# Gated attention and ReGLU block: the down products on exact 32-bit operands in four column tiles

## The chip, the cores and the metric

The kernel runs on one core of a Trainium2 chip. The metric is the time of one execution on the device in microseconds (us), the median of several runs. Five engines work side by side, each with its own instruction queue: PE (TensorE, matrix products; its weight loads are listed apart as PEld), DVE (VectorE), ACT (ScalarE), POOL (GpSimd) and SP (SyncE, which here only issues transfers). They meet through semaphores.

## The reference

For 2048 tokens of width 448 the result mixes an attention block (16 heads of width 28) and a gated feed-forward block (width 1792), token by token:

```python
x = A_x                                            # 1 x 2048 x 448
g = sigmoid((x * gate_w).sum(-1, keepdims=True))
qkv = (x @ wqkv).reshape(B, S, 3, H, Dh)           # H = 16, Dh = 28
p = softmax(einsum("bhqd,bhkd->bhqk", q, k) * Dh ** -0.5)
a = einsum("bhqk,bhkd->bhqd", p, v) ... @ wo
gate = einsum("bsd,df->bsf", x, W_gate)            # 448 -> 1792
up = einsum("bsd,df->bsf", x, W_up)
h = where(gate > 0, gate, 0) * up
b = einsum("bsf,fd->bsd", h, W_down)               # 1792 -> 448: the down products
out = g * a + (1 - g) * b
```

All arrays are 32-bit floats.

## The kernel before

The order of the instructions on every engine is written out by hand; no scheduler moves anything. The program has three stages.

**First stage.** Projections to q, k, v and the token gate, with x spilled to DRAM (`x_d`).

**Attention.** 32 rounds, two for each head. Each round follows a string of letters (`R0` to `R31`, listed in `ROUNDS`): `s` a pair of score products, `m` a pair of products for the row maxima, `x` one product of the feed-forward's gate or up projection (tile `gu`), `P` and `Q` the two halves of the products of P with V (function `pv`, tile `po`), and so on. `pv` works in *column tiles*: the stationary operand is a 128x32 piece of V, and four such products, one for each block of 512 tokens, write the partition rows 0 to 31, 32 to 63, 64 to 95 and 96 to 127 of one PSUM tile. P and V are 32-bit floats (F32) there. The feed-forward is spread under the attention: for every i (14 blocks f of 128 of the 1792 hidden columns, times 4 token blocks tb of 512; i = tb * 14 + f) the hidden tile h is computed as 128 hidden columns x 512 tokens and spilled to DRAM (`h_d`). The letter `D`, four times in the last two rounds, calls `split_wd`.

**Last stage** (after `stk.close()`). Four gate/up units that are left (`gate_up`), then for i = 0 to 55 the down products `down(i)`, accumulated over f into four PSUM tiles `ACC[tb][t]` of 128 tokens x 448; between them the output projection of the attention (`wout`, 11 products for each of the 16 token tiles t) and at each token block's end `result`, which mixes both parts and sends them out. A list `todo` sets the order of all engines here.

Most products use a *split*: an operand is divided into a high part, rounded to the type F32R, and the remainder (low), also F32R, and the product is formed as high x high, high x low, low x high. For the down products the table is

```python
PARTS = [(0, 0), (0, 1), (1, 0)]
```

so each (i, t) is three products of 128x128 stationary (h, one part) with 128x448 moving (weights, one part). The splits are extra work: `split_d(i)` makes `HH[i]` from the h tile (ACT the high part, line 136; DVE the low part, line 142), `split_wd(f)` does the same for the weights (ACT line 136, POOL line 145). The weights 0 to 3 are loaded and split early, in the last attention rounds, into the tiles K1 and K2; the weights 4 to 13 are fetched into `wdr` (4 places) by `fetch_w` and split into the tile `WD`. The h tiles 0 to 3 are also fetched early (tile `hk`, function `early_d`), the others by `fetch_h` into `hr` (4 places). All these fetches are issued by SP in program order. SP's issues use eight completion semaphores in turn, so an issue also waits until the transfer eight issues before it has landed.

Of the kernel before, what the change touches and what calls it, by code (L numbers as in the profile page):

```python
# [8 lines left out]
F32 = mybir.dt.float32  # L9
F32R = mybir.dt.float32r  # L10
# [8 lines left out]
P = 128  # L19
S = 2048  # L20
D = 448
H = 16
# [4 lines left out]
NF = F // P  # L27
NB = 4
TB = 512
# [62 lines left out]
QP = NL * NB * NT  # L92

BY_CHUNK = sorted(TERMS, key=lambda t: t[1] % 4)

PARTS = [(0, 0), (0, 1), (1, 0)]


@with_exitstack
def gated_mix_kernel(ctx, tc, x, wq, wo, wgu, wd, out):  # L100
    nc = tc.nc
# [7 lines left out]
    def f32(ap):  # L109
        return ap.bitcast(F32)  # L110
# [21 lines left out]
    def ps_x(name):  # L132
        return psum.tile([P, TB], F32, tag="x", bufs=2, name=name)

    def act_high(dst, src):
        nc.scalar.activation(dst, src, AF.Copy)  # L136
# [4 lines left out]
    def low(dst, src, high):  # L141
        nc.vector.tensor_tensor(dst, src, f32(high), op=OP.subtract)  # L142

    def pool_low(dst, src, high):
        nc.gpsimd.tensor_tensor(dst, src, f32(high), op=OP.subtract)
# [16 lines left out]
    V = vp.tile([P, 4, NK, 4, 32], F32, name="V")  # L162
    K = [(keep if r else vp).tile([P, S], F32R, name=f"K{r}") for r in range(3)]
# [42 lines left out]
    def rows_of(h):  # L206

        return [0 if j in raw(2 * h) else 1 if j in raw(2 * h + 1) else 2 for j in range(NB)]

    NU = [4 * sum(n > 0 for n in rows_of(h)) for h in range(H)]  # L210
    maxima = [(h, u, half) for h in range(H) for u in range(NU[h]) for half in range(rows_of(h)[u // 4])]
# [48 lines left out]
    stream = [p for v in range(2 * H) for p in visit(v)]  # L260
# [104 lines left out]
    with tc.tile_pool(name="qkv", bufs=1) as pa:  # L365
# [170 lines left out]
        m, first, ahead = 0, 6, MAXIMA  # L536
# [59 lines left out]
    done = (starts[-1] - QP) // (2 * NT)  # L596
# [127 lines left out]
        for j in range(4):  # L724
            nc.sync.dma_start(wo_d.rearrange("(g j d) n -> j d g n", j=4, d=DH)[j], wo[32 * j:32 * j + DH])

    DR, HK, early = {}, {}, []

    def wd_high_low(f, b):

        if f < 4:
            return K[1 + f // 2][:, (2 * (f % 2) + b) * D:(2 * (f % 2) + b + 1) * D]
        return WD[0][:, f - 4, b]

    def early_d():

        for i in range(0, 4, 2):
            h = fe.tile([P, 2, 4, P], F32, name=f"hk_{i}", tag="wgr", bufs=2).rearrange("p s c f -> p (s c f)")
            for k in range(2):
                DR[i + k] = V[:, 0].rearrange("p k h d -> p (k h d)")[:, (i + k) * D:(i + k + 1) * D]  # L740
                HK[i + k] = h[:, k * TB:(k + 1) * TB]
                nc.sync.dma_start(DR[i + k], wd[(i + k) * P:(i + k + 1) * P])
                nc.sync.dma_start(HK[i + k], h_d[i + k])

    def split_wd(i):

        r = DR.pop(i)
        act_high(wd_high_low(i, 0), r)
        pool_low(wd_high_low(i, 1), r, wd_high_low(i, 0))

    WD = []
    parts = 0
    passes = [(*divmod(k, 2), n) for k in range(-NL * NB, 2 * done) for n in range(NT)]
# [3 lines left out]
    def small_things(u):  # L757

        h, q = divmod(u, 4)

        if u in (22, 38):
            g = 2 if u < 32 else 3
            nc.sync.dma_start(V[:, g % 2], v_d[g])
        if u == 2:
            pack_wo()
        if h and q == 1:
            row_sums(h - 1)
            spread(h - 1)

    def loads(h, load):  # L770

        if 2 < h + 2 < H:
            load(h + 2)

    for v, order in enumerate(ROUNDS):
        small_things(2 * v)
        if v == 2 * H - 3:
            early_d()
        ns = 0
        for o in order:  # L780
            if o == "s":
                ns += 1
                if ns == 6:
                    small_things(2 * v + 1)
                if ns in (1, 9) and v % 2 == 0:
                    loads(v // 2, load_k if ns == 1 else load_q)
                if stream:
                    score()
            elif o == "m":
                if m < len(maxima):  # L790
                    smax(m)
                    m += 1
            elif o == "x":
                i, half, n = passes.pop(0)
                u = 2 * i + half + NL * NB
                if n == 0:
                    units.append(ps_x(f"qk_{u}" if i < 0 else f"gu_{i}_{half}"))
                if i < 0:
                    qk_mm(units[-1], u, n)
                else:  # L800
                    gu_mm(units[-1], i, half, n)
                if n == NT - 1:
                    ps = units.pop()
                    if half:
                        finished.add(i)
                    if i < 0:
                        send_qk(ps, NE + u % NL, u // NL, nc.sync)
                    elif half:
                        load_f(i + 2)
                        spill_h(i, ps)  # L810
                    else:
                        relu(i, ps)
            elif o == "n":
                if v % 2 and v < 2 * H - 1:
                    smax_end(v // 2 + 1)
            elif o == "w":
                ready = -(-max(0, starts[v + 2] - QP) // NT)
                ready = min(ready + ready % 2, 2 * NF)
                while parts < ready and parts // 2 - 2 in finished:
                    split_f(parts // 2, act_high, pool_low, (parts % 2,))  # L820
                    parts += 1
                    if parts % 2 == 0:
                        fetch_f(parts // 2 + 1)
            elif o == "b":
                block_min()
            elif o == "A":
                all_max()
            elif o == "g":
                take_max()
            elif o == "N":  # L830
                if v > 1 and v % 2:
                    normalise(v // 2 - 1)
            elif o in "eE":
                take_exp(o == "E")
            elif o in "cf":
                rescale(v, "cf".index(o))
            elif o == "D":
                split_wd(len(early))
                early.append(o)
            elif o in "PQ":  # L840
                pv(v, "PQ".index(o))
        rest = [k for k in todo_exp + todo_sub + todo_all if k[0] == v]
        assert not rest and v not in PO or len(stream) == max(0, 16 * (2 * H - 1 - v) - AHEAD), (v, passes, rest, len(stream) + 16 * (v + 1))
    assert not stream and not passes and m == len(maxima) and len(early) == 4, (len(stream), len(passes), m)
    stk.close()


# [1 line left out]
    pf = ctx.enter_context(tc.tile_pool(name="ffn", bufs=1))  # L849
# [12 lines left out]
        act_high(WO[:, 6], r[:, 3])  # L862
        low(WO[64:, 6], r[64:, 3], WO[64:, 6])

    ON, OR, GA, HH, ACC = {}, {}, {}, {}, {}

    def fetch_o(tb):
        OR[tb] = r = pf.tile([P, 4, TB], F32, name=f"or_{tb}", tag="or", bufs=1)
# [32 lines left out]
        relu(i, ps[:, 0])  # L901
        spill_h(i, ps[:, 1])

    WD.append(pf.tile([P, NF - 4, 2, D], F32R, name="WD"))

    def fetch_w(i):

        if i < NF:
            DR[i] = pf.tile([P, D], F32, name=f"wdr_{i}", tag="wdr", bufs=4)
            nc.sync.dma_start(DR[i], wd[i * P:(i + 1) * P])  # L910

    def fetch_h(i):

        if i < NB * NF:
            HK[i] = pf.tile([P, TB], F32, name=f"hr_{i}", tag="hr", bufs=4)
            nc.sync.dma_start(HK[i], h_d[i])

    def split_d(i):
        HH[i] = pf.tile([P, 2, TB], F32R, name=f"hh_{i}", tag="hh", bufs=3)
        h = HK.pop(i)  # L920
        act_high(HH[i][:, 0], h)
        low(HH[i][:, 1], h, HH[i][:, 0])

    def down_mm(i, t):
        f = i % NF
        for n, (a, b) in enumerate(PARTS):
            nc.tensor.matmul(ACC[i // NF][t][:, :D], HH[i][:, a, t * P:(t + 1) * P], wd_high_low(f, b),  # L927
                             start=(f == 0 and n == 0), stop=(f == NF - 1 and n == 2))

    def result(tb, t, queue):  # L930
        k = tb * 4 + t
# [8 lines left out]
    def down(i):  # L940
# [6 lines left out]
        if f == NF - 1:  # L947
# [5 lines left out]


    wor = []
    todo = [(fetch_w, 4), (fetch_h, 4), (fetch_w, 5), (fetch_h, 5), (split_d, 0), (row_sums, H - 1), (split_d, 1),
            (fetch_w, 6), (fetch_w, 7), (lambda: wor.append(load_wo()),), (fetch_h, 6), (gate_up, done), (spread, H - 1),
            (split_wd, 4), (fetch_w, 8), (split_wd, 5), (fetch_w, 9), (fetch_h, 7), (gate_up, done + 1)]
    for i in range(NB * NF):
        if 5 < i + 3 < NF:  # L960
            todo += [(split_wd, i + 3), (fetch_w, i + 7)]
        if i + 2 < NB * NF:
            todo.append((split_d, i + 2))
        if i >= 2:
            todo.append((fetch_h, i + 6))
        todo.append((down, i))
        if i % 2 == 0 and 2 < i and done + i // 2 < NB * NF:
            todo.append((gate_up, done + i // 2))
# [54 lines left out]
```

## Time and profile before

| | before |
|---|---|
| median of 3 runs | 1184.81 us (1184.59 to 1185.01) |
| profiled execution, its own time | 1184.21 us |
| its span, first to last instruction | 1182.4 us |
| granted TensorE clock, mean | 0.999 |
| DMA, mean over the span | 160 GB/s |
| last stage, from the first `gate_up` product to the last down product | 985.76 to 1178.6 us |

The span is what the trace's rows add up to; the execution's own time is 1.8 us more, before the first and after the last instruction. In the page and in the answers on the trace, "PE MATMUL acc<-WD,hh 128*128 128x448 f32 x480 | 99.5, 366" means: 480 products that write tile acc from tiles WD and hh, stationary 128x128, moving 128x448, together busy 99.5 us, one lasting 366 ns from its start to its end. Products overlap in the pipeline, so the pace is read from the starts of successive ones in the timeline and not from that duration.

### The profile page before, as it was taken

The page shows a single profiled execution, that of the slowest core. Times are in us where ns is not written, and L with a number is a line of the kernel's source. Part 1 is how long each engine was busy: PE and PEld are TensorE (multiplying, and loading weights), DVE is VectorE, ACT ScalarE, POOL GpSimd, SP SyncE. Part 2 cuts the span into 40 slices and gives each one's busy share as a digit, 9 for nine tenths or more (in the row PEclk, how much of TensorE's full clock was granted, in tenths as well). Part 3 has the DMA queues.
Part 4 walks back from the last instruction along what each step waited for, and adds up shares of the span by engine and source line. Part 5 has one row for each costly group of instructions (what it writes and reads, how often), then busy time and mean ns, then how long its engine had stood idle before and what let it go on. Part 6 is the DMA issues. An engine that isn't in the chain of part 4 may idle for free.

```text
span 1182.4 us, 17006 instructions
## 1 busy us (share of the span) xinstructions
PE 1175.0 (99%) x6183; PEld 821.2 (69%) x6183; DVE 894.1 (76%) x1173; ACT 877.2 (74%) x1054; POOL 743.3 (63%) x325
## 2 busy tenths in 40 slices
PE   9999999999999999999999999999999999999998
PEld 6886666666666666666666666666666667899997
DVE  6577898888988898989898888889898553444242
ACT  5237889899999988888888887888888885322121
POOL 5323667888988886777777766767676784422020
PEclk9999999999999999999999999999999999999999
DMA  9994565636373754343446535153444437644342
GB/s 322 280 394 142 186 210 172 185 124 196 117 216 108 205 167 139 119 128 92 119 136 212 140 102 153 49 152 109 139 154 156 129 100 231 209 152 118 115 134 75
DMA packets 70667, 188.85 MB, mean 160 GB/s; under 512 B 13958, under 2 KB 20558, under 8 KB 65678
## 3 DMA queue, kind: packets, MB, share of 16 engines
q1 hardware_dynamic: 65624, 167.31, 45.9%
q0 software_dynamic: 4480, 19.99, 4.5%
q8 instruction: 48, 0.79, 0.3%
q10 hardware_dynamic: 480, 0.47, 0.1%
q14 instruction: 35, 0.29, 0.1%
HBM read 126.96 MB, written 60.96 MB: 159 GB/s over the span
## 4 chain that ended last, share of the span: by engine, by line
PE 96%; DVE 1%; DMA 1%; ACT 1%; issue 0%; SPq 0%; DVEq 0%; ACTq 0%
PE gu L633 24%; PE s L330 20%; PE po L692 19%; PE acc L927 12%; PE sm L224 10%; PE v L469 3%; PE wo L886 3%; PE qk L641 3%; PE qk L454 2%; DVE r L280 1%; DMA wr<-wq 0%; DMA X<-x_d 0%; ACT P L336 0%; ACT V L336 0%; SPq L414 0%
## 5 line engine op out<-in xcount | busy, mean ns | idle before, releaser
L309 POOL TENSOR_TENSOR P<-P,rm 128x2048 f32<-128x2048 f32 x102 | 470.8, 4635 | 107.9 <-DVE rm L303 84.1
L633 PE MATMUL gu<-X,wg 128*128 128x512 f32 x1232 | 358.9, 395 | 0.1
L228 DVE TENSOR_REDUCE mx<-sm 128x1 f32<-128x1024 f32 x256 | 302.9, 1217 | 43.0 <-PE sm L224 42.1
L330 PE MATMUL s<-Q,K 128*128 128x512 f32 x1024 | 315.9, 403 | 1.7 <-DVE mx L228 0.9
L633 PEld LDWEIGHTS gu<-X,wg 128*128 128x128 f32 x1232 | 231.2, 188 | 57.6 <-issue 1.7
L330 PEld LDWEIGHTS s<-Q,K 128*128 128x128 f32 x1024 | 180.7, 188 | 82.4 <-DVE r L280 10.4
L336 ACT ACTIVATE P<-s 128x1024 f32<-128x1024 f32 x204 | 202.2, 1028 | 42.0 <-PE s L330 39.6
L692 PE MATMUL po<-P,V 128*32 128x512 f32 x1640 | 227.4, 594 | 0.0
L334 ACT ACTIVATE P<-s 128x1024 f32<-128x1024 f32 x206 | 201.4, 1040 | 14.1 <-PE s L330 13.1
L320 ACT ACTIVATE P<-P 128x1024 f32<-128x1024 f32 (+1 forms) x182 | 208.5, 1171 | 0.5 <-POOL P L309 0.2
L224 PE MATMUL sm<-K,Q 128*128 128x512 f32 x520 | 163.2, 400 | 0.1
L280 DVE SCALAR_TENSOR_TENSOR r<-s,r 128x1024 f32<-128x1024 f32 x124 | 151.6, 1223 | 13.6 <-ACT P L336 6.0
L692 PEld LDWEIGHTS po<-P,V 128*32 128x32 f32 x1640 | 62.6, 110 | 113.3 <-issue 109.6
L692 PE MATMUL po<-V 128*32 128x512 f32 x408 | 136.2, 594 | 0.0
L309 POOL TENSOR_TENSOR V<-V,rm 128x2048 f32<-128x2048 f32 x24 | 111.2, 4635 | 26.1 <-DVE rm L303 22.6
L224 PEld LDWEIGHTS sm<-K,Q 128*128 128x128 f32 x520 | 91.9, 188 | 34.1 <-ACT P L334 4.6
L136 ACT ACTIVATE hh<-hr 128x512 fp32r<-128x512 f32 x52 | 32.8, 632 | 109.5 <-PE acc L927 109.4
L142 DVE TENSOR_TENSOR hh<-hr,hh 128x512 fp32r<-128x512 f32 x52 | 47.3, 915 | 72.6 <-ACT hh L136 72.5
L927 PE MATMUL acc<-WD,hh 128*128 128x448 f32 x480 | 99.5, 366 | 0.0
L927 PEld LDWEIGHTS acc<-WD,hh 128*128 128x128 f32 x480 | 90.2, 188 | 7.3 <-DVE hh L142 0.2
L280 DVE SCALAR_TENSOR_TENSOR r<-s,P 128x1024 f32<-128x1024 f32 x50 | 61.1, 1223 | 33.3 <-ACT P L336 33.0
L295 DVE TRANSPOSE_TENSOR_REDUCE mn<-r 128x32 f32<-128x1024 f32 x63 | 78.1, 1239 | 1.3
(93 smaller groups left out, 1135.5 us busy)
## 6 DMA issues: line engine op xcount, KB each, us to landing
wg<-ws_d SPq DMA_DIRECT2D x42, 896.0 KB
K<-qk_d SPq DMA_DIRECT2D x32, 448.0 KB
X<-x_d SPq DMA_DIRECT2D x56, 256.0 KB
h_d<-h SPq DMA_DIRECT2D x56, 256.0 KB
Q<-qk_d SPq DMA_DIRECT2D x62, 224.0 KB
hr<-h_d SPq DMA_DIRECT2D x52, 256.0 KB
ws_d<-wg SPq DMA_DIRECT2D x14, 896.0 KB
x_d<-X POOLq DMA_DIRECT2D x8, 1024.0 KB, 15.2
```

Of the source, the lines that this page charges most:

```text
L224: nc.tensor.matmul(ps[:, c, :], Q[h][:, u * P:(u + 1) * P], K[h % 3][:, k0:k0 + TB], start=True, stop=True)
L228: nc.vector.tensor_reduce(to, ps, axis=AX.XY, op=OP.max)
L280: nc.vector.scalar_tensor_tensor(r, ps, -1.0, before, op0=OP.mult, op1=OP.min)
L295: nc.vector.tensor_reduce(MN[:, 1:3], R2.pop((v, j)).rearrange("p a (b r) -> p a b r", r=32), axis=AX.X, op=OP.min, apply_transpose=True)
L309: nc.gpsimd.tensor_tensor(QUAD[q], QUAD[q], m, op=OP.subtract)
L320: nc.scalar.activation(q, q, AF.Exp, scale=-SCALE)
L330: nc.tensor.matmul(ps[:, c], K[h % 3][:, k * P:(k + 1) * P], Q[h][:, j * TB:(j + 1) * TB], start=True, stop=True)
L334: nc.scalar.activation(dst, ps, AF.Exp, scale=SCALE)
L336: nc.scalar.activation(dst, ps, AF.Copy, scale=-1.0)
L633: nc.tensor.matmul(ps, WS[i][:, s, a], xf(i // NF, b), start=(n == 0), stop=(n == NT - 1))
L692: nc.tensor.matmul(po[32 * j:32 * j + 32], V[:, h // 4 % 2, k, h % 4], AT.pop((v, k, j)), start=(k == k0), stop=(k == k0 + NK // 2 - 1))
L927: nc.tensor.matmul(ACC[i // NF][t][:, :D], HH[i][:, a, t * P:(t + 1) * P], wd_high_low(f, b), start=(f == 0 and n == 0), stop=(f == NF - 1 ...
```

## The change

Both operands of the down products stay whole 32-bit floats (F32). Nothing is split: `PARTS`, `split_d`, `split_wd` and the tiles `HH` and `wdr` are gone. Each (i, t) becomes four products, one for each group of 32 tokens, with a 128x32 stationary piece of h and the 128x448 moving weights of block f; they write the partition rows 0, 32, 64 and 96 onwards of the same PSUM tile. The weights 0 to 3 are no longer fetched in the attention rounds; all 14 are fetched straight into `WD` in the last stage, 0 to 3 first of all. `hr` has eight places where there were four.

```diff
-PARTS = [(0, 0), (0, 1), (1, 0)]
...
-    def wd_high_low(f, b):
-
-        if f < 4:
-            return K[1 + f // 2][:, (2 * (f % 2) + b) * D:(2 * (f % 2) + b + 1) * D]
-        return WD[0][:, f - 4, b]
+    def wd_rows(f):
+
+        return WD[0][:, f]
...
-                DR[i + k] = V[:, 0].rearrange("p k h d -> p (k h d)")[:, (i + k) * D:(i + k + 1) * D]
                 HK[i + k] = h[:, k * TB:(k + 1) * TB]
-                nc.sync.dma_start(DR[i + k], wd[(i + k) * P:(i + k + 1) * P])
                 nc.sync.dma_start(HK[i + k], h_d[i + k])
-
-    def split_wd(i):
-
-        r = DR.pop(i)
-        act_high(wd_high_low(i, 0), r)
-        pool_low(wd_high_low(i, 1), r, wd_high_low(i, 0))
...
-            elif o == "D":
-                split_wd(len(early))
-                early.append(o)
...
-    WD.append(pf.tile([P, NF - 4, 2, D], F32R, name="WD"))
+    WD.append(pf.tile([P, NF, D], F32, name="WD"))
...
-            DR[i] = pf.tile([P, D], F32, name=f"wdr_{i}", tag="wdr", bufs=4)
-            nc.sync.dma_start(DR[i], wd[i * P:(i + 1) * P])
+            nc.sync.dma_start(wd_rows(i), wd[i * P:(i + 1) * P])
...
-            HK[i] = pf.tile([P, TB], F32, name=f"hr_{i}", tag="hr", bufs=4)
+            HK[i] = pf.tile([P, TB], F32, name=f"hr_{i}", tag="hr", bufs=8)
...
-    def split_d(i):
-        HH[i] = pf.tile([P, 2, TB], F32R, name=f"hh_{i}", tag="hh", bufs=3)
-        h = HK.pop(i)
-        act_high(HH[i][:, 0], h)
-        low(HH[i][:, 1], h, HH[i][:, 0])
 
     def down_mm(i, t):
         f = i % NF
-        for n, (a, b) in enumerate(PARTS):
-            nc.tensor.matmul(ACC[i // NF][t][:, :D], HH[i][:, a, t * P:(t + 1) * P], wd_high_low(f, b),
-                             start=(f == 0 and n == 0), stop=(f == NF - 1 and n == 2))
+        for k in range(0, P, 32):
+            nc.tensor.matmul(ACC[i // NF][t][k:k + 32, :D], HK[i][:, t * P + k:t * P + k + 32], wd_rows(f), start=(f == 0),
+                             stop=(f == NF - 1))
...
-    todo = [(fetch_w, 4), (fetch_h, 4), (fetch_w, 5), (fetch_h, 5), (split_d, 0), (row_sums, H - 1), (split_d, 1),
+    todo = [(fetch_w, 0), (fetch_w, 1), (fetch_w, 2), (fetch_w, 3), (fetch_w, 4), (fetch_h, 4), (fetch_w, 5), (fetch_h, 5), (row_sums, H - 1),
...
-            todo += [(split_wd, i + 3), (fetch_w, i + 7)]
-        if i + 2 < NB * NF:
-            todo.append((split_d, i + 2))
+            todo.append((fetch_w, i + 7))
```

On PE the same place in the program, `down(1)`, reads as follows; `acc_0` to `acc_3` are the four PSUM tiles of the token block, `hh` the split h, `K_105` the early split weights. Before:

```order
L927 MATMUL acc_0_9059<-K_105,hh_8966 128x448 [waits Activation_49]
L927 MATMUL acc_0_9059<-K_105,hh_8966 128x448
L927 MATMUL acc_0_9059<-K_105,hh_8966 128x448 [waits DVE_49]
L927 MATMUL acc_1_9060<-K_105,hh_8966 128x448 x3
L927 MATMUL acc_2_9061<-K_105,hh_8966 128x448 x3
L927 MATMUL acc_3_9062<-K_105,hh_8966 128x448 x3
```

With the change (`hk` is the unsplit h tile, fetched early):

```order
L905 MATMUL acc_0_9032<-WD,hk_8257 32x448 [waits DMAHW1_49]
L905 MATMUL acc_0_9032<-WD,hk_8257 32x448 x3
L905 MATMUL acc_1_9033<-WD,hk_8257 32x448 x4
L905 MATMUL acc_2_9034<-WD,hk_8257 32x448 x4
L905 MATMUL acc_3_9035<-WD,hk_8257 32x448 x4
```

Twelve products that waited for ACT and DVE have become sixteen narrow ones that wait only for the weights' transfer.

On SP's queue the start of the last stage is reordered; `ls` is the last head's row sums, `l_d` sends them back, `wor` is the output projection's weights. Before:

```order
L702 DMA ls_8939<-ox 128x1x16 [waits DMAHW3_49,DVE_49]
L910 DMA wdr_8952<-wd 128x448 [waits DMAHW4_49,PE_49,Pool_49]
L916 DMA hr_8954<-h_d_2606 128x512 [waits DMAHW5_49]
L910 DMA wdr_8956<-wd 128x448 [waits DMAHW6_49]
L916 DMA hr_8958<-h_d_2768 128x512 [waits DMAHW7_49]
L708 DMA l_d_97<-rq_8963 128x16 [waits DMAHW0_49,DVE_49]
```

With the change:

```order
L700 DMA ls_8927<-ox 128x1x16 [waits DMAHW7_49,DVE_49]
L894 DMA WD<-wd 128x448 [waits DMAHW0_49,PE_49,Activation_49]
L894 DMA WD<-wd 128x448 [waits DMAHW1_49]
L894 DMA WD<-wd 128x448 [waits DMAHW2_49]
L894 DMA WD<-wd 128x448 [waits DMAHW3_49]
L894 DMA WD<-wd 128x448 [waits DMAHW4_49]
L900 DMA hr_8945<-h_d_2606 128x512 [waits DMAHW5_49]
L894 DMA WD<-wd 128x448 [waits DMAHW6_49]
L900 DMA hr_8948<-h_d_2768 128x512 [waits DMAHW7_49]
L706 DMA l_d_97<-rq_8950 128x16 [waits DMAHW0_49,DVE_49]
```

Four weight transfers stand ahead of everything that was there. The first waits for PE, that is for the last product of P with V, whose operand V lay where `WD` now begins.

More of the change, by code (lines that the diff above doesn't have):

```diff
@@ L725, in pack_wo @@
             nc.sync.dma_start(wo_d.rearrange("(g j d) n -> j d g n", j=4, d=DH)[j], wo[32 * j:32 * j + DH])
-    DR, HK, early = {}, {}, []
-    def wd_high_low(f, b):
-        if f < 4:
-            return K[1 + f // 2][:, (2 * (f % 2) + b) * D:(2 * (f % 2) + b + 1) * D]
-        return WD[0][:, f - 4, b]
+    HK = {}
+    def wd_rows(f):
+        return WD[0][:, f]
     def early_d():
@@ L843, in gated_mix_kernel @@
         assert not rest and v not in PO or len(stream) == max(0, 16 * (2 * H - 1 - v) - AHEAD), (v, passes, rest, len(stream) + 16 * (v + 1))
-    assert not stream and not passes and m == len(maxima) and len(early) == 4, (len(stream), len(passes), m)
+    assert not stream and not passes and m == len(maxima), (len(stream), len(passes), m)
     stk.close()
@@ L863, in split_wo @@
         low(WO[64:, 6], r[64:, 3], WO[64:, 6])
-    ON, OR, GA, HH, ACC = {}, {}, {}, {}, {}
+    ON, OR, GA, ACC = {}, {}, {}, {}
     def fetch_o(tb):
@@ L955, in gated_mix_kernel @@
     wor = []
-    todo = [(fetch_w, 4), (fetch_h, 4), (fetch_w, 5), (fetch_h, 5), (split_d, 0), (row_sums, H - 1), (split_d, 1),
+    todo = [(fetch_w, 0), (fetch_w, 1), (fetch_w, 2), (fetch_w, 3), (fetch_w, 4), (fetch_h, 4), (fetch_w, 5), (fetch_h, 5), (row_sums, H - 1),
             (fetch_w, 6), (fetch_w, 7), (lambda: wor.append(load_wo()),), (fetch_h, 6), (gate_up, done), (spread, H - 1),
-            (split_wd, 4), (fetch_w, 8), (split_wd, 5), (fetch_w, 9), (fetch_h, 7), (gate_up, done + 1)]
+            (fetch_w, 8), (fetch_w, 9), (fetch_h, 7), (gate_up, done + 1)]
     for i in range(NB * NF):
         if 5 < i + 3 < NF:
-            todo += [(split_wd, i + 3), (fetch_w, i + 7)]
-        if i + 2 < NB * NF:
-            todo.append((split_d, i + 2))
+            todo.append((fetch_w, i + 7))
         if i >= 2:
```

## The prediction

> **What bounds the kernel now.** I read the page's busy shares and the chain first. The chain is the work that ended last, followed back; its second row splits its share by line.
>
> ```profile
> PE 1175.0 (99%) x6183; PEld 821.2 (69%) x6183; DVE 894.1 (76%) x1173; ACT 877.2 (74%) x1054; POOL 743.3 (63%) x325
> ...
> PE 96%; DVE 1%; DMA 1%; ACT 1%; issue 0%; SPq 0%; DVEq 0%; ACTq 0%
> PE gu L633 24%; PE s L330 20%; PE po L692 19%; PE acc L927 12%; PE sm L224 10%; PE v L469 3%; PE wo L886 3%; PE qk L641 3%; PE qk L454 2%; DVE r L280 1%; DMA wr<-wq 0%; DMA X<-x_d 0%; ACT P L336 0%; ACT V L336 0%; SPq L414 0%
> ```
>
> PE is the chain nearly throughout, and the down products (`acc`, line 927) are 12% of it. Since an average can hide a stage with another limit, I then asked for busy time in two stretches, the last stage and all before it; the columns are length, then each engine's busy time and instructions, clock, DMA share and GB/s.
>
> ```profile
> 985.76:1178.60 192.84, 192.81 (x940) 175.86 (x936) 78.43 (x100) 51.34 (x81) 38.90 (x31) 1.00 0.48 150
> 0.00:985.76 985.76, 982.20 (x5248) 645.39 (x5248) 815.02 (x1072) 825.87 (x973) 704.41 (x295) 1.00 0.51 162
> ```
>
> In the last stage PE is busy 192.81 of 192.84 us, at a granted clock of 1.00; DVE is busy 78.43 and ACT 51.34 of these. So whatever changes PE's work there changes the end by as much, and work taken from DVE, ACT or POOL gives nothing. Before that stage PE lacks 3.56 us in all, so taking the four early splits away can give at most that and, as the splits are 8 small instructions among thousands, I take 0. The last question is how long PE takes for a product of each kind.
>
> **The products that go.** The groups by line, with their shapes, give the count: 480 + 192 = 672 products of 128x448.
>
> ```profile
> L927 PE MATMUL acc<-WD,hh 128*128 128x448 f32 x480 | 99.5, 366 | 0.0
> L927 PE MATMUL acc<-K,hh 128*128 128x448 f32 x192 | 39.6, 365 | 0.0
> ...
> L142 DVE TENSOR_TENSOR hh<-hr,hh 128x512 fp32r<-128x512 f32 x52 | 47.3, 915 | 72.6 <-ACT hh L136 72.5
> L136 ACT ACTIVATE hh<-hr 128x512 fp32r<-128x512 f32 x52 | 32.8, 632 | 109.5 <-PE acc L927 109.4
> ```
>
> The pace stands in the timeline (start, time covered, engine, count), where down products alternate with the equally shaped `wo` products:
>
> ```profile
> 1059.16 2.40 PE L886 MATMUL wo<-WO,on 128*128 128x448 f32 x11
> 1061.40 2.60 PE L927 MATMUL acc<-WD,hh 128*128 128x448 f32 x12
> 1063.83 2.39 PE L886 MATMUL wo<-WO,on 128*128 128x448 f32 x11
> ```
>
> From 1059.16 to 1063.83 PE starts 23 products: 4.67 / 23 = 0.203 us each. Gone from PE: 672 x 0.203 = **136.4 us**. The splits of h go too (52 x 0.632 on ACT, 52 x 0.915 on DVE, and four more of each for the early tiles), but both groups' idle columns show the splits waiting, ACT for PE and DVE for ACT: they run ahead of PE and were never what it waited for. Their gain is 0.
>
> **The products that come.** 56 h tiles x 4 token tiles x 4 column tiles = 896 products of 128x32 stationary with 128x448 moving, both 32-bit. The trace has their like: the products of P with V are 128x32 with 128x512, both F32, four column tiles in turn. One line's view, and one `P`+`Q` run in the timeline from the product before it to the one after:
>
> ```profile
> L692 PEld LDWEIGHTS po<-P,V x1640: 105/110/111, 114.0 to 984.8; 128*32 128x32 f32 x183
> L692 PE MATMUL po<-P,V x1640: 592/592/618, 114.0 to 985.2; 128*32 128x512 f32 x183
> L692 PEld LDWEIGHTS po<-V x408: 106/110/111, 117.0 to 984.8; 128*32 128x32 f32 x136
> L692 PE MATMUL po<-V x408: 592/592/617, 117.4 to 985.2; 128*32 128x512 f32 x136
> ...
> 617.73 0.62 PE L330 MATMUL s<-Q,K 128*128 128x512 f32 x2
> 618.19 0.39 PE L633 MATMUL gu<-X,wg 128*128 128x512 f32 x1
> ...
> 620.13 1.08 PE L330 MATMUL s<-Q,K 128*128 128x512 f32 x4
> 621.15 0.62 PE L692 MATMUL po<-P,V 128*32 128x512 f32 x2
> ...
> 621.61 0.59 PE L692 MATMUL po<-V 128*32 128x512 f32 x1
> ...
> 627.61 0.61 PE L692 MATMUL po<-P,V 128*32 128x512 f32 x3
> ...
> 628.15 1.20 PE L330 MATMUL s<-Q,K 128*128 128x512 f32 x4
> ```
>
> The code has 32 visits x 8 k x 4 j = 1024 such products; the view counts 1640 + 408 = 2048, so the hardware runs each 32-bit product as two loads and two products. In the timeline they come in sets of four records, one for each column tile, side by side; a visit's half-head has 64 records, 16 sets, and the first starts at 621.15 and the last at 627.61: 6.46 / 15 = 0.431 us a set (neighbouring sets show 0.43). Four products of 512 columns thus take two sets, 0.861 us.
>
> How this shrinks to 448 columns the trace does not show. If a set is streaming of its columns, it becomes 0.431 x 448 / 512 = 0.377; if it is a fixed cost (loads, issue), it stays 0.431. The full-array products decide which is nearer: 512 columns take (618.19 - 617.73) / 2 = 0.230, 448 take 0.203, which is 0.88 of it against 448 / 512 = 0.875. Time goes with columns there, and a set of 0.431 is two passes of 512 at 0.215, a little under the full array's 0.230, so it has even less fixed cost. I take **0.377**. The lower bound is the pace without the first set, 627.61 - 621.61 over 14 or less, 0.428 x 0.875 = 0.375; the upper is 0.431.
>
> 224 (i, t) x 2 sets x 0.377 = **168.9 us**, with bounds 168.0 and 193.1.
>
> A rule of the Trainium skill, page "FP8 and Floating Point Precision", section TensorE Precision Notes, bears on this: a true FP32 product takes 4 passes through the array. The trace agrees, as two sets of 0.431 are four times 0.215. Priced with the full array's pass of 448 instead, that rule gives 224 x 4 x 0.203 = 181.9 and so 13 us more; since the column-tiled pass is measured the shorter, the set stands.
>
> **Switching between full array and column tiles.** Into the run: four `s` from 620.13 at 0.230 would be over at 621.05, and `po` starts at 621.15, 0.10 later. Out of it: the last set's start plus 0.431 is 628.04, the next product starts at 628.15, 0.11 later. In the program the down products stand in 13 unbroken pieces: 13 x 0.10 + 12 x 0.11 = **2.6 us**, which were not there (the alternation at 1061.40 shows no such gap). Bounds 0 and twice that.
>
> **The moved loads.** Rows 0 to 3 of the weights are now fetched in the last stage, behind the row sums `ls`; the first waits for the last product with V. Order and landing of the like before:
>
> ```profile
> 985.76 3.07 PE L633 MATMUL gu<-X,wg 128*128 128x512 f32 x12
> ...
> 986.84 0.61 SPq L702 DMA_DIRECT2D ls<-ox  x1
> 987.55 0.41 SPq L910 DMA_DIRECT2D wdr<-wd  x1
> ...
> 996.17 1.18 PE L927 MATMUL acc<-K,hh 128*128 128x448 f32 x5
> ...
> wdr<-wd SPq DMA_DIRECT2D x10, 224.0 KB
> ...
> L136 ACT ACTIVATE WD<-wdr x10: 559/567/579, 991.7 to 1029.1; 128x448 fp32r<-128x448 f32 x10
> ...
> 986.20:996.20 10.00, 10.00 (x45) 8.04 (x44) 2.79 (x5) 2.79 (x5) 3.39 (x3) 1.00 0.94 315
> ```
>
> PV ends and `gate_up` begins at 985.76, so that wait is over before `ls` is issued; row 0 takes the place of the transfer issued at 987.55, which was used at 991.7 at the latest. PE needs it at 996.17: 4.5 us to spare, hidden by the two `gate_up`. Rows 1 to 3 follow in four issues of 0.41 to 0.47 and are needed 3 us apart. What is queued behind is later by 4 x 224 KB at 315 GB/s, about 2.9 us: the h tiles 4 and 5, `l_d`, `wor`, the weights of the third `gate_up`, which PE needs only after `down(4)`. There PE also arrives later, by 5 x (2 x 4 x 0.377 - 12 x 0.203) = 2.9 us, as much as the transfers. Cost 0; if the cover failed, at most some 4 us (a transfer queued wholly behind, and its landing). The eight places of `hr` are refilled when a `down` has freed one, so h is fetched six `down`, some 18 us, ahead, and a fetch has no longer to wait for a split.
>
> **The end.** The last product, one DVE mix and one transfer are as before:
>
> ```profile
> 1178.61 0.68 DVE L933 SCALAR_TENSOR_TENSOR y<-acc,gate,ga 128x448 f32<-128x448 f32 x1 [0.53 <-PE acc L927]
> 1179.32 0.36 ACTq L935 DMA_DIRECT2D out<-y  x1
> ```
>
> DVE needs 0.68 for a token tile; PE gives it one each 1.22 now and each 4 x 0.377 = 1.51 then. Nothing is added.
>
> **Sum.** -136.4 + 168.9 + 2.6 = +35.1 us. On the profiled execution's own time, 1184.21 (span 1182.4), that is 1219.3; the median of the runs is 0.6 higher, 1184.81, which gives **1219.9 us**.
>
> **The rivals.**
>
> *The sets do not shrink.* A set is held at 0.431 by something that does not go with columns. The widths above speak against it, though no 448-column set is in the trace. 193.1 + 2.6 - 136.4 = +59.3: 1244. Between lies a set whose passes each pay the full array's 0.203: 448 x 2 x 0.203 = 181.9, +48.1, 1233.
>
> *The weight loads come out from under the products.* A set needs four loads of 0.110 (row above). If one such time were exposed in each set because here each column tile has other weights, while the four tiles of PV load the same piece of V: 448 x 0.110 = 49.3 more, 1269. The timeline speaks against it: the loads are made in PV too, and 0.431 leaves no room beside two passes' worth of streaming. The Trainium skill, page "TensorE: Matmul & The Clock Gate", section The mechanism, states that weight loads overlap running products only where the row groups differ. By that rule all column tiles, which share their rows, would expose their loads; the PV sets, 0.431 with loads of 0.110 in it, do not bear it out, and I give it little.
>
> *A transfer is late at the start of the stage*, by the 4 us above: 1224.
>
> *Faster.* The four tiles of a set read the same weights here and four different tiles of P in PV. If PV's pace were that of reading its moving operands, a shared one could go up to four times as fast. It decides from 136.4 - 2.6 = 133.8 / 448 = 0.299 us a set down; at half the pace, 0.19, the sum is 85.1 + 2.6 - 136.4 = -48.7, 1136. Against it: a pass of 512 takes 0.215 there, while the full array, with one moving operand, takes 0.230; PV is not slower than one stream, so a shared one has nothing to gain.
>
> **How the numbers follow.** Sets that shrink with the columns, everything hidden: 0.83. Late transfer: 0.04. No shrinking, or the full array's pass: 0.07. Exposed loads: 0.02. Faster: 0.03; something that balances it: 0.01. 0.2%, 2.4 us, is about what a measurement of this kernel can tell from no change. So slower 0.96, same 0.01, faster 0.03. The range: below, the set at 0.375, no switching cost and the 3.56 us of early idle returned, -136.4 + 168.0 - 3.56 = +28.0, 1212.8; above, the forecast with switching doubled, the late transfer and half of the way to the full array's pass, 1219.9 + 2.6 + 4 + 6.5 = 1233.
>
> **What would show it.** The line of the down products should count 1792 records of 128x32, in sets 0.377 apart, 3.02 us for one `down`, and the last stage should last 192.8 + 35.1 = 228 us. Sets at 0.43 show the second case; sets near 0.49 the loads; a gap on PE ahead of the first `down` or of the third `gate_up` the transfers. ACT and DVE should be nearly idle there. The prediction is wrong if a set is not what a set in PV is: same form, but other weights in each tile and one moving operand for all four.

## The result and the profile after

The changed kernel takes 1221.85 us, median of 4 runs (1220.68 to 1222.16), against 1184.91 us (1184.59 to 1186.27) for the kernel before in the same set of runs: a ratio of 1.0308 (1.029 to 1.0326), 36.9 us more. The forecast was 1219.9 us. The profiled execution after took 1220.68 us with a span of 1218.8 us, 36.4 us more than the span before.

The page's busy times, and the chain by engine and by line:

```profile
span 1218.8 us, 19006 instructions
...
PE 1211.4 (99%) x7303; PEld 750.6 (62%) x7303; DVE 844.6 (69%) x1117; ACT 836.5 (69%) x984; POOL 723.4 (59%) x311
...
PE 96%; ACT 1%; DVE 1%; DMA 1%; issue 0%; SPq 0%; ACTq 0%; DVEq 0%
PE gu L631 23%; PE s L328 19%; PE po L690 18%; PE acc L905 14%; PE sm L222 10%; PE wo L871 3%; PE v L467 3%; PE qk L639 3%; PE qk L452 2%; DVE r L278 1%; DMA wr<-wq 0%; ACT P L334 0%; DMA v_d<-V 0%; ACT P L332 0%; ACT V L334 0%
```

DVE lost 49.5 us of work, ACT 40.7, POOL 19.9, and none of it came back in the time: PE was the chain before and is the chain after, and PE's busy time rose by 36.4 us, from 1175.0 to 1211.4, as much as the span. The down products' share of the chain rose from 12% to 14%. The windows of the last stage, and of its first five `down`, show no hole on PE, and PE's own list of waits in this stage has no row (columns: length, then busy time of PE, PEld, DVE, ACT and POOL with their instructions, clock, DMA share, GB/s):

```profile
985.56:1214.40 228.84, 228.84 (x2060) 105.50 (x2056) 29.10 (x44) 12.30 (x15) 21.95 (x19) 1.00 0.41 130
996.06:1011.23 15.17, 15.17 (x161) 5.10 (x160) 3.48 (x6) 2.50 (x4) 1.28 (x1) 1.00 0.98 326
```

The answer on the line of the down products has 1664 + 128 = 1792 records, as forecast:

```profile
L905 PE MATMUL acc<-WD,hr x1664: 539/539/564, 1008.1 to 1214.4; 128*32 128x448 f32 x185
L905 PE MATMUL acc<-WD,hk x128: 539/539/563, 996.1 to 1007.8; 128*32 128x448 f32 x128
```

The timeline around one `down` between two `wo` runs gives the pace. The four weight loads that go with a set show when the set starts:

```profile
1035.62 1.69 PE L905 MATMUL acc<-WD,hr 128*32 128x448 f32 x16
1037.24 2.50 PE L871 MATMUL wo<-WO,on 128*128 128x448 f32 x11
1039.67 3.21 PE L905 MATMUL acc<-WD,hr 128*32 128x448 f32 x32
1042.82 0.47 PE L871 MATMUL wo<-WO,on 128*128 128x448 f32 x1
...
1040.07 0.13 PEld L905 LDWEIGHTS acc<-WD,hr 128*32 128x32 f32 x4 [0.25 <-issue]
1040.45 0.13 PEld L905 LDWEIGHTS acc<-WD,hr 128*32 128x32 f32 x4 [0.25 <-issue]
1040.82 0.13 PEld L905 LDWEIGHTS acc<-WD,hr 128*32 128x32 f32 x4 [0.25 <-issue]
```

From 1040.07 to 1040.82 there are two sets; in the trace's nanoseconds they start 0.376 apart (0.377 was forecast). The `down` from 1039.67 to 1042.82 takes 3.15 us, 0.14 more than its eight sets of 0.376, and the run of 11 `wo` from 1037.24 to 1039.67 takes 2.43 us where 11 x 0.203 = 2.23 were needed before. So each change from full array to column tiles and back costs 0.20 + 0.14 = 0.34 us, where 0.21 was forecast.

### The profile page after: what moved, and what is told of

The parts are those of the page before. It is cut to its first block, busy times and chain, and to the rows that moved or that the text cites. A ratio compares the mean times of both kernels' runs of the same rounds, so it can differ in the third digit from the quotient of the medians.

```text
span 1218.8 us, 19006 instructions
## 1 busy us (share of the span) xinstructions
PE 1211.4 (99%) x7303; PEld 750.6 (62%) x7303; DVE 844.6 (69%) x1117; ACT 836.5 (69%) x984; POOL 723.4 (59%) x311
## 4 chain that ended last, share of the span: by engine, by line
PE 96%; ACT 1%; DVE 1%; DMA 1%; issue 0%; SPq 0%; ACTq 0%; DVEq 0%
PE gu L631 23%; PE s L328 19%; PE po L690 18%; PE acc L905 14%; PE sm L222 10%; PE wo L871 3%; PE v L467 3%; PE qk L639 3%; PE qk L452 2%; DVE r L278 1%; DMA wr<-wq 0%; ACT P L334 0%; DMA v_d<-V 0%; ACT P L332 0%; ACT V L334 0%
## 5 line engine op out<-in xcount | busy, mean ns | idle before, releaser
L905 PE MATMUL acc<-WD,hr 128*32 128x448 f32 x1664 | 159.0, 540 | 0.0
L905 PEld LDWEIGHTS acc<-WD,hr 128*32 128x32 f32 x1664 | 52.8, 110 | 100.2 <-issue 99.2
L134 ACT ACTIVATE on<-or 128x1024 fp32r<-128x1024 f32 x8 | 8.1, 1052 | 111.8 <-DMA or<-o_d 111.8
L911 DVE SCALAR_TENSOR_TENSOR y<-acc,gate,ga 128x448 f32<-128x448 f32 x16 | 10.8, 683 | 95.8 <-PE acc L905 95.3
```

Of the source, the lines that this page charges most:

```text
L905: nc.tensor.matmul(ACC[i // NF][t][k:k + 32, :D], HK[i][:, t * P + k:t * P + k + 32], wd_rows(f), start=(f == 0), stop=(f == NF - 1))
```

## The experiments

Six kernels ran: the changed one again, and five variants of it. The theory: the down products cost what they stream, eight sets of 0.376 us for each `down` instead of twelve products of 0.203, plus a price for each change between full array and column tiles; nothing else in the change moves the time. The rivals: the moved transfers, the splits that are gone, the column tiles as such, weight loads, the places for h.

**The changed kernel beside the variants** (no edit).

> The changed kernel unaltered, timed beside the other variants on the same chip. Every theory expects 1221.9 us, give or take 1, and the down products in sets 0.376 us apart.

1222.06 us, median of 5 runs, ratio to the kernel before 1.0306 (1.0292 to 1.032). It is what e1, e2 and e3, run on the same chip, are compared with.

**Only the products put back.** (Lines not shown here declare the tiles of h as F32R.)

```diff
-        for k in range(0, P, 32):
-            nc.tensor.matmul(ACC[i // NF][t][k:k + 32, :D], HK[i][:, t * P + k:t * P + k + 32], wd_rows(f), start=(f == 0),
-                             stop=(f == NF - 1))
+        for n in range(3):
+            nc.tensor.matmul(ACC[i // NF][t][:, :D], HK[i][:, t * P:(t + 1) * P], K[1][:, n * D:(n + 1) * D],
+                             start=(f == 0 and n == 0), stop=(f == NF - 1 and n == 2))
```

> Everything of the change stays (weights fetched in the last stage, eight places for h, no split of h or weights), but each (i, t) is again three one-pass F32R products of 128x128 with 128x448. Left out: the low parts (h is rounded to F32R where it is made) and the weights themselves, in whose place the products read a stale tile of the same shape, so that they wait for h's transfers but not for the weights'. Theory (the loss lies in PE's products alone, and the splits were hidden): the time of the kernel before, 1184.9, within 1 us. Rival 1 (the moved fetches and the new order of SP's queue cost a part of it): 1187 or more. Rival 2 (the splits did cost PE something, which their absence gives back and the products hide): 1183 or less.

1185.32 us, ratio 0.9998 (0.9989 to 1.0006). The timeline has the old pace back, 23 products from 1059.68 to 1064.34, 0.203 each, and no gap at the changes:

```profile
1059.68 2.39 PE L871 MATMUL wo<-WO,on 128*128 128x448 f32 x11
1061.90 2.60 PE L905 MATMUL acc<-K,hr 128*128 128x448 f32 x12
1064.34 2.39 PE L871 MATMUL wo<-WO,on 128*128 128x448 f32 x11
```

The whole loss lies in the products. Both rivals fall as far as this kernel can tell: the moved fetches cost nothing, and neither did the splits, which are absent here without any gain. That a cost and a gain cancel is not what PE shows: it is busy for 1174.8 us, against 1175.0 before. One thing this kernel leaves out: its products do not wait for the weights' transfers. That those were in time is seen in the changed kernel itself, whose window 996.06 to 1011.23 has PE busy 15.17 of 15.17 us.

**The same 32-bit products on the full array.**

```diff
-        for k in range(0, P, 32):
-            nc.tensor.matmul(ACC[i // NF][t][k:k + 32, :D], HK[i][:, t * P + k:t * P + k + 32], wd_rows(f), start=(f == 0),
-                             stop=(f == NF - 1))
+        nc.tensor.matmul(ACC[i // NF][t][:, :D], HK[i][:, t * P:(t + 1) * P], wd_rows(f), start=(f == 0), stop=(f == NF - 1))
```

> The changed kernel with one 32-bit product of 128x128 with 128x448 per (i, t) in place of the four column tiles. Theory (a 32-bit product is four passes over its columns, tiles or not): 224 x 4 passes at 0.188 (the pass of a set here) to 0.203 (the full array's one-pass product) = 168.4 to 181.9 us, no switching, against 136.2 before: 1217 to 1231; likeliest two passes and one fixed cost of 16 ns, 174.4, 1223. Rival 1 (the column tiles themselves are what costs): the full array's 32-bit product takes under 0.70 us, under 1206. Rival 2 (the column tiles hide weight loads that the full array can't hide, two of 0.188 per product): 224 x (0.752 + 0.376) = 252.7, 1301.

1217.47 us, ratio 1.0267 (1.0253 to 1.0281), 4.6 us less than the changed kernel. It lies at the lower end of the expected range; the 1223 called likeliest, with a fixed cost for each record, was too high. By form, and in the timeline:

```profile
L904 PE MATMUL acc<-WD,hr 128*128 128x448 f32 x416 | 158.4, 539 | 0.0
L904 PEld LDWEIGHTS acc<-WD,hr 128*128 128x128 f32 x416 | 79.0, 190 | 73.3 <-issue 72.1 <-DVE y L909 0.4 <-DVE ga L878 0.4
...
1038.47 2.73 PE L871 MATMUL wo<-WO,on 128*128 128x448 f32 x11
1041.04 3.17 PE L904 MATMUL acc<-WD,hr 128*128 128x448 f32 x8
1043.69 0.71 PE L871 MATMUL wo<-WO,on 128*128 128x448 f32 x1
```

A record on the full array (two per product here too, 56 x 4 x 2 = 448) lasts 539 ns, exactly like one in a column tile, and it does the work of a set of four. `wo` and `down` together take 5.22 us (1038.47 to 1043.69); 11 x 0.203 + 8 x 0.376 = 5.24. (Only the two together can be read this way: the first `wo` record of a run is shown from before the last `down` is through, so the run of `wo` looks 0.34 too long and the `down` as much too short.) So the records follow at 0.376, as the sets do, and no price is paid at the changes. Four column tiles side by side are as fast as one full array, not faster: cutting 128 tokens into four times 32 gained nothing. The changes, 4.2 us as worked out below, are nearly all that this kernel is faster by. Neither rival holds.

**Fewer changes between the two.**

```diff
-for tb, load, split, at in ((0, 4, (7, 8), (10, 11, 12, 13)), (1, 10, (15, 16), (18, 19, 20, 21)), (2, 21, (23, 25), (28,) * 4),
+for tb, load, split, at in ((0, 4, (7, 8), (13,) * 4), (1, 10, (15, 16), (21,) * 4), (2, 21, (23, 25), (28,) * 4),
```

> The changed kernel, but the output projection of the token blocks 0 and 1 stands in one run of four token tiles each (before down 13 and down 21), as it already does for the blocks 2 and 3: 7 unbroken pieces of down products in place of 13. Theory (each change from the full array to column tiles and back costs 0.33 us, read from the trace of the changed kernel: the first wo product of a run 0.11 late, the second 0.11, the first set 0.09 and 0.02): 6 x 0.33 = 2.0 us less than the changed kernel, 1219.9. Rival (these gaps are waits for PSUM tiles or for operands of the output projection, which lie at these places anyway): the same time, 1221.9, with as many gaps.

1219.65 us, ratio 1.0285 (1.0271 to 1.0299), 2.4 us under the changed kernel's 1222.06 (2.0 expected). The run of 44 `wo` lasts 9.12 us, 0.19 more than 44 x 0.203 = 8.93, as much as a single run of 11 loses:

```profile
1047.23 9.19 PE L871 MATMUL wo<-WO,on 128*128 128x448 f32 x44
1056.35 2.09 PE L905 MATMUL acc<-WD,hr 128*32 128x448 f32 x20
```

Thirteen pieces, seven and none give 1222.06, 1219.65 and 1217.47: 0.40 and 0.31 us for a piece less, on either side of the 0.34 read above; no run of one of the three kernels overlaps with a run of the next. Had the gaps been waits for the operands of each `wo` tile, they would have moved along with the tiles; the 44 products stand without a gap.

**Four places for h.**

```diff
-            HK[i] = pf.tile([P, TB], F32, name=f"hr_{i}", tag="hr", bufs=8)
+            HK[i] = pf.tile([P, TB], F32, name=f"hr_{i}", tag="hr", bufs=4)
```

> The changed kernel with four places for h in place of eight. A fetch then waits for the down three further on, so h comes three downs (9 us) ahead and not six, and what is queued behind it on SP waits too. Theory (h's fetches are far ahead of PE either way, and PE's products set the time): 1222, within 1.5 us of the changed kernel. Rival (the eight places are what keeps PE fed once no split stands between fetch and product): 1225 or more, with gaps on PE before downs.

1222.15 us, ratio to the kernel before 1.031 (1.0293 to 1.0328), like the changed kernel's. The waits of SP's queue, first the changed kernel's row, then this one's:

```profile
SPq L900 <- PE acc L905: 138.5, 41, 12.0
```

```profile
SPq L900 <- PE acc L905: 161.2, 48, 12.0
```

The fetches wait 48 times for PE instead of 41, and PE does not notice: its own list of waits in this stage has no row in either kernel. The eight places are not what keeps PE fed.

**Narrow products.**

```diff
-            nc.tensor.matmul(ACC[i // NF][t][k:k + 32, :D], HK[i][:, t * P + k:t * P + k + 32], wd_rows(f), start=(f == 0),
+            nc.tensor.matmul(ACC[i // NF][t][k:k + 32, :P if f else D], HK[i][:, t * P + k:t * P + k + 32], wd_rows(f)[:, :P if f else D], start=(f == 0),
```

> The changed kernel with the down products cut to 128 of their 448 columns, except for f = 0 (16 of the 224 pairs keep 448 columns); the other columns' sums are left out. It asks from what width on a set is no longer its columns. Theory (a set is two passes of its columns and nothing else, loads hidden): 0.376 x 128 / 448 = 0.107 to 0.110 a set; 208 x 2 x (0.376 - 0.109) = 111 us less than the changed kernel, 1111. Rival 1 (the four loads of 0.110 need their time once it isn't covered, one after the other behind the products): 0.22 a set or more, 1157 or more. Rival 2 (the fixed cost that is hidden at 448 columns is the issue of four loads and four products, somewhere between): 0.13 to 0.2 a set, 1120 to 1149.

1124.57 us in a single run, 13.6 above the theory's 1111. By the total this lies in the second rival's band; the trace says otherwise. A `down` that stands alone, in the timeline and in a window of its own:

```profile
1052.28 1.08 PE L905 MATMUL acc<-WD,hr 128*32 128x128 f32 x32
1053.29 0.30 PEld L871 LDWEIGHTS wo<-WO,on 128*128 128x128 f32 x2 [0.20 <-issue]
...
1028.22:1029.23 1.01, 1.01 (x33) 0.81 (x32) 0.90 (x2) 0.00 (x0) 0.00 (x0) 1.00 1.05 325
```

Eight sets and the change out take 1.01 us; less 0.14, a set takes 0.109 as the theory had it, with four loads of 0.110 each hidden under it. In the trace's nanoseconds the sets of the long stretches start 0.109 apart too, but for those behind a wait. What the theory missed is elsewhere: PE's waits in the last stage, which no other kernel here has, and two windows (the clock is the third column from the end):

```profile
PE wo L871 <- ACT on L134: 2.4, 2, 1.9
PE wo L871 <- POOL on L143: 2.3, 2, 1.6
PE gu L631 <- DVE gate L583: 2.1, 1, 2.1
PE acc L905 <- issue: 1.5, 2, 0.9
PE acc L905 <- DVE y L911: 1.0, 1, 1.0
...
1005.51:1008.92 3.41, 3.41 (x10) 2.63 (x9) 0.00 (x0) 0.00 (x0) 1.28 (x1) 0.50 0.97 306
1094.26:1097.66 3.40, 3.40 (x11) 3.01 (x10) 0.00 (x0) 0.00 (x0) 1.31 (x3) 0.50 0.74 270
```

ACT's and POOL's splits for `wo`, and DVE, now end waits of PE: a PE that needs 111 us less in this stage loses its cover, and waits for 9.3 us in all. Only the 1.5 us under "issue" have no name. Around these waits the granted clock fell to 0.50 for 3.4 us, twice, and the products there started 0.43 apart instead of 0.23, and 0.37 instead of 0.20, which is some 3 us more. Together that is about 12 of the 13.6 us; the sets have no part in it.

## Why the prediction was right, and what it mis-sized

*What goes: 136.4 us.* This held: with the three products back and the rest of the change kept, the time is the old one (e1).

*What comes: 168.9 us.* This held: 448 sets at 0.376 are 168.4. The choice between "a set shrinks with its columns" and "a set keeps its 0.431" was right, and e5 carries it down to 128 columns. No 448-column set was in the old trace, but PV's set and the two widths of full-array products were enough. (The 0.230 for 512 columns came from two products; the median over all successive `gu` products is 0.232, which makes the ratio of the two widths 0.875, exactly that of their columns.)

*Switching: 2.6 us.* This term was too small; it is about 4.2 us (12 changes at 0.34 and one more entry at 0.12). The forecast took the time to the first product on either side, 0.10 and 0.11. It missed that the second full-array product also comes 0.11 late and the second set 0.02. The fence of the prediction had the row for it: four `s` ahead of PV cover 1.08 us, four behind it 1.20. With 4.2, the sum is 168.4 - 136.4 + 4.2 = 36.2, against the span's 36.4. So 1.3 of the 2.0 us between forecast and median are this sum's; the rest lies in the step from the profiled execution to the median of the runs, 0.6 before and 1.2 after.

*Moved loads: 0.* This held: the first `down` starts at 996.06 (996.17 before) and PE is busy throughout the next 15.17 us. *Splits: 0.* This held: 110 us of work of three engines went, and e1 without them is no faster than the kernel before. *Eight places: 0.* This held too (e4).

*The rivals.* Sets at 0.431, full-array passes, exposed loads and a shared stream would have shown as a set of 0.43, 0.41, 0.49 and under 0.30: it is 0.376. For the exposed loads, the Trainium skill (page "TensorE: Matmul & The Clock Gate", section The mechanism) has loads overlap running products only where row groups differ. The four tiles here share all rows; their loads of 0.110 are hidden in sets of 0.376, and in e5 even in sets of 0.109, shorter than one load. The measurement decides against that rule for column tiles. The same section of the Trainium skill also has a load run ahead where it goes to a background weight buffer, which these numbers do not contradict.

No version with the whole result beats the kernel before. The best with 32-bit operands is the full array's, 32 us behind: two records of 0.376 for a product against three of 0.203.

## What to carry to other kernels

Count PE's own time for each way to form the product: here two records of 0.376 us for 32-bit operands, against three products of 0.203 for the split into high and low parts. What ACT, DVE and POOL pay for the split does not count as long as it is hidden; e5 shows that the cover ends when PE gets much faster. Cutting a full stationary operand of 128 into four column tiles of 32 gained nothing here and added the price of changing over. Read that price behind the change too, not only to the first product.

## What the runs showed of the hardware that was not expected

Counted as two passes, as the prediction does, a 32-bit record takes less for each pass over 448 columns than an F32R product: 0.376 / 2 = 0.188 against 0.203 on the same full array (e2 and e1). So the split's advantage is not 4 to 3 but 0.752 to 0.609. Why an F32R product carries some 0.015 us more is open; each one has its own load of 0.188, while the 32-bit product has one load for two passes, but no run separates this.

In e5 the granted clock fell to 0.50 for 3.4 us twice, about 1 us after PE had started again: once behind a single wait of 2.1 us, once behind three waits of together 4.2 us within 7 us. Two waits of about 1 us that stood alone were not followed by it. In the other kernels, whose PE has no wait in this stage, the clock stays at 1.00 there. What exactly triggers it was not tried.
